# The second expert choice of a routed layer, searched by counting keys on TensorE in 7 rounds

## The chip, the cores and the metric

One core of a Trainium2 chip runs the whole program. The time is the device time of one execution in microseconds (us), as the median of several. The engines are TensorE (PE, with its weight loads shown as PEld), VectorE (DVE), ScalarE (ACT), GpSimd (POOL) and SyncE (SP, which issues most of the transfers). Each engine works through its own instructions strictly in the order in which the program wrote them, and waits on semaphores for the others.

## The reference

Three layers follow each other. Only the second one's choice of tokens matters here.

```python
# attention without softmax, then RMS norm: x of 4608 tokens x 512
logits = x @ w_gate                       # 4608 x 8
order = np.argsort(-logits.flatten())     # all token-expert pairs, best first
for idx in order:
    tok, e = idx // E, idx % E
    if assigned[tok] >= 0 or counts[e] >= cap:   # cap = 4608 / 8 = 576
        continue
    assigned[tok] = e; counts[e] += 1
for e in range(8):
    out[assigned == e] = relu(x[assigned == e] @ w1[e]) @ w2[e]
# third layer, for all tokens: max of three products (each with a relu), then w_out
```

Each expert gets exactly 576 tokens. The kernel never sorts: it settles one expert per "route", eight routes in a row. A route gives every free token its best expert among those still open, finds for each expert how many tokens lie above a threshold, and searches the threshold at which the first expert fills up. That expert takes its tokens and is closed.

## The kernel before

Attention comes first (0 to about 116 us), for all tokens, and leaves the normed tokens in DRAM as `xd` with the logits in SBUF as `L`. Then come eight expert stages. A stage p gathers the 576 tokens of one expert, transposes them, and runs on them w1 (8 tiles of 128 rows, 2 halves of 288 columns), w2 (4 x 2 x 2 halves), the three weights of the third layer (6 x 2 halves x 3) and finally w_out. Every float32 product is made as three matmuls of split operands (function mm3, lines 888 to 890), so a half is 12 matmuls of 288 columns.

Route p+1 runs inside stage p, as a Python generator `phase(p + 1)`. After each half of 12 matmuls the stage calls `tick()`. A tick advances the generator from one `yield` to the next, and so puts a piece of the route's instructions into the queues between two halves. A stage has 68 ticks (the first one 67). `drain()` at its end writes what is left. The order of the instructions on each engine is thus set by where the yields stand. A yield between an instruction on DVE and the one on PE that reads its result gives the DVE a tick's time.

The first stage does one thing more. Its weights of the third layer and w_out arrive as 64-bit words. A second generator, `decoder()`, turns them into float32 pairs, 24 tiles, one piece a tick from the fifth tick on: per tile two ACT casts (lines 367, 368), a shift and a merge on DVE (372, 379), an addition on POOL (380), a cast on ACT (386 or 388) and a subtraction on DVE (394) or POOL (394, 397). The six tiles of w_out are written back to DRAM (`wod`, line 398), and their places then take the last six tiles by a load on SP (line 355). The list `ready` grows to 24 when all is decoded. The buffers `xg` hold both the decoder's values and the gathered tokens, so `tick()` gathers only when `ready` has 24.

The first route (phase 0, before the first stage) searches in `top_search`: DVE compares the keys of all 4608 tokens with 63, 31 or 15 thresholds at once (lines 329, 581, 583), TensorE multiplies the one-hot matrix of experts with these 0/1 columns, 36 pairs of weight load and matmul, and so counts the tokens of each expert above every threshold. A second small matmul spreads the outcome. That takes 7 rounds.

Routes 1 to 6 use `search` (line 504); the last route takes what is left and searches nothing. The keys are first transposed on TensorE (lines 718 to 726) to 96 rows of an expert and a third of the columns. A round has three thresholds. ACT takes two as sums of signs (line 512), DVE the third (514); DVE combines them (518), TensorE sums over rows (523, one small matmul), and DVE compares with the places left and moves the threshold (527 to 534). There are 11 rounds on the upper part of the key, then a change of keys (735 to 743), then 5 rounds on the lower part. A round has two yields, in route 1's first eight rounds three (`slow`).

After the search, `finish` turns the choice into 576 row numbers (IDX; its 36 pairs on TensorE are line 656), `gather` issues five indirect transfers on POOL (line 862), `scale` multiplies the gathered rows with the norm on POOL (868), and `trans` transposes them on TensorE (877). The scaling stands at the stage's end, the transposes among the matmuls of w_out (1044 to 1046), from their second sixth on.

Of the kernel before, what the change touches and what calls it, by code (L numbers as in the profile page):

```python
# [9 lines left out]
F32 = mybir.dt.float32  # L10
F32R = mybir.dt.float32r
BF = mybir.dt.bfloat16
# [11 lines left out]
E = 8  # L24
# [8 lines left out]
J0 = 63  # L33
# [4 lines left out]
def body(ctx: ExitStack, tc: tile.TileContext, qx, kx, vx, g, wg, w1, w2, w123, wo, out):  # L38
# [98 lines left out]
    th0 = ac.tile([128, J0], F32, name="th0")  # L137
    nc.vector.tensor_scalar(th0, d1[:, 1:J0 + 1], 2.0 ** 18, None, op0=OP.mult)
    STEPS = ((2 ** 13, 31), (2 ** 8, 31), (2 ** 4, 15), (1, 15), (16, 15), (1, 15))
    TH = ac.tile([128, 6, 31], F32, name="TH")  # L140
    SV = ac.tile([128, 7], F32, name="SV")
# [361 lines left out]

    def search(KT, i0, i1, REM2, slow):

        T = SC[:, i0]
        for i in range(i0, i1):
# [12 lines left out]
            if slow and i < 8:  # L520
                yield
# [24 lines left out]
    def top_search(g2):  # L546
# [44 lines left out]
        return commit(g2, K, 1.0, OH0)  # L591

# [85 lines left out]

    def phase(p):
# [19 lines left out]
        else:  # L699
# [7 lines left out]
            sf, hi, lo = keys(best, 10)  # L707
            nc.vector.tensor_tensor(sf, sf, hi, op=OP.add)
            nc.vector.tensor_mul(sf, sf, AL)
# [3 lines left out]
            KT = []  # L713
            for i, key in enumerate((sf, best)):
                K = V.rearrange("p e c -> p (e c)").rearrange("p (g e c) -> p g e c", g=3, e=E)
                for g in range(3):
                    gs = slice(12 * g, 12 * g + 12)
                    nc.vector.tensor_mul(K[:, g], oh[:, :, gs], key[:, None, gs].to_broadcast([128, E, 12]))
                yield
                yield  # L720
                pt = rps.tile([128, 512], F32, name="rps")
                for g in range(3):
                    nc.tensor.transpose(pt[0:96, g * 128:g * 128 + 128], K[:, g].rearrange("p e c -> p (e c)"),
                                        ident)
                KT.append(rt.tile([128, 384], F32, name="KT", tag="KT" + str(i))[0:96])
                nc.scalar.copy(KT[i], pt[0:96, 0:384])
                yield
            b1 = None
            for r in search(KT[0], 0, 11, REM2, p == 1):
                if r is None:  # L730
                    yield
                else:
                    b1 = r
            H1 = rt.tile([128, 1], F32, name="H1")
            nc.vector.tensor_scalar(H1, b1, 0.5, None, op0=OP.max)
            nc.vector.scalar_tensor_tensor(KT[1], KT[0], H1[0:96], KT[1], op0=OP.is_equal, op1=OP.mult)
            yield
            nc.vector.tensor_scalar(KT[0], KT[0], H1[0:96], 3000.0, op0=OP.is_gt, op1=OP.mult)
            nc.vector.tensor_add(KT[0], KT[0], KT[1])
            t = rt.tile([128, NT], F32, name="kt")  # L740
            nc.vector.scalar_tensor_tensor(t, sf, H1, best, op0=OP.is_equal, op1=OP.mult)
            nc.vector.tensor_scalar(sf, sf, H1, 3000.0, op0=OP.is_gt, op1=OP.mult)
            nc.vector.tensor_add(sf, sf, t)
            yield
            b2 = None
            for r in search(KT[0], 11, 16, REM2, False):
                if r is None:
                    yield
                else:
                    b2 = r  # L750
            L1 = rt.tile([128, 1], F32, name="L1")
            nc.vector.tensor_scalar(L1, b2, 1.0, None, op0=OP.add)
            flags = commit(g2, sf, L1, oh)
# [158 lines left out]
    beat = 0  # L912

    def tick():
# [183 lines left out]
```

## Time and profile before

| | |
|---|---|
| median of 3 runs | 1275.76 us (1274.73 to 1277.25) |
| profiled execution | 1274.72 us, span 1272.9 us |
| busy PE, DVE, ACT, POOL | 1208.8, 646.0, 482.3, 398.2 us |
| first stage, first matmul of its second half to last of the third layer's | 161.97 to 302.65 us |
| the same stretch, busy PE and DVE | 120.78 and 118.66 us |

Busy time of PE counts matmuls with modelled ends. [...] An idle time in the profile is put down to the instruction that released it. The span lies 1.8 us inside the profiled execution's own time, and that execution is 1.04 us below the median.

### The profile page before, as it was taken

How to read it: one execution, taken by the hardware profiler on the slowest of the kernel's cores; microseconds unless marked ns; L12 is line 12 of the kernel's file. 1: busy time of each engine (PE TensorE's matmuls, PEld its weight loads, DVE VectorE, ACT ScalarE, POOL GpSimd, SP SyncE). 2: the span in 40 equal slices, each digit the busy share in tenths (PEclk: the TensorE clock that was granted, in tenths of full speed). 3: DMA queues.
4: the chain of work that ended last, by engine and by line, in shares of the span. 5: the costliest groups of instructions: out<-in, count | busy, mean ns of one | idle time of the engine just before them, and what ended most of it. 6: DMA issues, size and time to landing. Idle time of an engine off the chain costs nothing.

```text
span 1272.9 us, 23272 instructions
## 1 busy us (share of the span) xinstructions
PE 1208.8 (95%) x8878; PEld 1136.6 (89%) x8880; DVE 646.0 (51%) x2075; ACT 482.3 (38%) x1166; POOL 398.2 (31%) x483
## 2 busy tenths in 40 slices
PE   9996698778999999999999999999999999999996
PEld 7885398777999989998999899999999899989995
DVE  2656688873576346653666167725763421121110
ACT  3547254651453136413542155314631331133110
POOL 0000123544521354135412451245214451253121
PEclk9998798889999999999999999999999999999998
DMA  9999410343330223121311232113312252023101
GB/s 342 396 380 355 150 59 25 118 148 105 109 100 26 80 75 109 34 94 54 102 65 59 64 117 84 59 47 108 100 35 70 76 161 86 1 75 109 59 1 42
DMA packets 52033, 136.15 MB, mean 107 GB/s; under 512 B 5840, under 2 KB 10448, under 8 KB 50384
## 3 DMA queue, kind: packets, MB, share of 16 engines
q1 hardware_dynamic: 44672, 110.25, 25.8%
q0 software_dynamic: 6944, 24.38, 5.7%
q8 instruction: 70, 1.15, 0.4%
q14 instruction: 43, 0.35, 0.1%
q10 hardware_dynamic: 304, 0.02, 0.0%
HBM read 111.43 MB, written 23.20 MB: 106 GB/s over the span
## 4 chain that ended last, share of the span: by engine, by line
PE 77%; DVE 12%; ACT 5%; issue 2%; DMA 2%; POOL 1%; POOLq 0%; SPq 0%; ACTq 0%; DVEq 0%
PE mm L888 19%; PE mm L890 18%; PE mm L889 18%; PE mm L1044 4%; PE mm L1046 4%; PE mm L1045 4%; PE kv L189 4%; ACT W L512 3%; PE o L225 2%; DVE T L534 2%; PE tp L877 1%; DVE w L394 1%; DVE w L379 1%; DVE dv L372 1%; DMA vtb<-vx_dram 1%
## 5 line engine op out<-in xcount | busy, mean ns | idle before, releaser
L888 PE MATMUL mm<-X,w 128*128 128x288 f32 x1152 | 346.9, 301 | 0.0
L890 PE MATMUL mm<-X,w 128*128 128x288 f32 x1152 | 341.3, 296 | 0.0
L889 PE MATMUL mm<-X,w 128*128 128x288 f32 x1152 | 341.2, 296 | 0.0
L888 PEld LDWEIGHTS mm<-X,w 128*128 128x128 f32 x1152 | 218.7, 190 | 0.4
L889 PEld LDWEIGHTS mm<-X,w 128*128 128x128 f32 x1152 | 218.2, 189 | 0.0
L890 PEld LDWEIGHTS mm<-X,w 128*128 128x128 f32 x1152 | 218.0, 189 | 0.0
L838 POOL TENSOR_TENSOR ring<-raw,ring 128x512 fp32r<-128x512 f32 x112 | 144.2, 1289 | 206.8 <-ACT ring L829 195.8
L1021 POOL TENSOR_TENSOR H<-t,H 128x288 fp32r<-128x288 f32 x96 | 77.8, 810 | 417.1 <-ACT H L1020 417.0
L1019 DVE TENSOR_TENSOR t<-mm,t 128x288 f32<-128x288 f32 x192 | 87.1, 454 | 159.5 <-PE mm L890 157.8
L888 PE MATMUL mm<-H,ring 128*128 128x288 f32 x512 | 156.5, 306 | 0.0
L888 PE MATMUL mm<-X,ring 128*128 128x288 f32 (+1 forms) x512 | 153.7, 300 | 1.6 <-ACT X L883 1.6
L889 PE MATMUL mm<-H,ring 128*128 128x288 f32 x512 | 152.3, 297 | 0.0
L890 PE MATMUL mm<-H,ring 128*128 128x288 f32 x512 | 152.1, 297 | 0.0
L890 PE MATMUL mm<-X,ring 128*128 128x288 f32 (+1 forms) x512 | 151.1, 295 | 0.6 <-DVE X L884 0.6
L889 PE MATMUL mm<-X,ring 128*128 128x288 f32 (+1 forms) x512 | 150.7, 294 | 0.0
L512 ACT ACTIVATE W<-KT,T 96x384 bf16<-96x384 f32 x168 | 102.1, 608 | 117.3 <-DVE T L534 117.3
L1020 ACT CAST H<-t 128x288 fp32r<-128x288 f32 x96 | 41.4, 432 | 231.6 <-DVE t L1019 231.6
L888 PEld LDWEIGHTS mm<-X,ring 128*128 128x128 f32 x512 | 96.4, 188 | 2.2 <-ACT X L883 2.1
L888 PEld LDWEIGHTS mm<-H,ring 128*128 128x128 f32 x512 | 98.0, 191 | 0.0
L889 PEld LDWEIGHTS mm<-H,ring 128*128 128x128 f32 x512 | 97.5, 190 | 0.0
L890 PEld LDWEIGHTS mm<-H,ring 128*128 128x128 f32 x512 | 97.2, 190 | 0.0
L890 PEld LDWEIGHTS mm<-X,ring 128*128 128x128 f32 x512 | 96.1, 188 | 1.1 <-DVE X L884 1.1
(257 smaller groups left out, 2037.4 us busy)
## 6 DMA issues: line engine op xcount, KB each, us to landing
raw<-w_dram SPq DMA_DIRECT2D x128, 256.0 KB, 2.7
ring<-wod SPq DMA_DIRECT2D x48, 512.0 KB, 3.5
xd<-y SPq DMA_DIRECT2D x36, 288.0 KB, 9.4
w<-w_dram SPq DMA_DIRECT2D x18, 512.0 KB, 8.2
qta<-qx_dram SPq DMA_DIRECT2D x4, 1280.0 KB, 15.0
qtb<-qx_dram SPq DMA_DIRECT2D x4, 1024.0 KB, 12.4
kta<-kx_dram SPq DMA_DIRECT2D x3, 1280.0 KB, 17.6
vta<-vx_dram SPq DMA_DIRECT2D x3, 1280.0 KB, 16.6
```

Of the source, the lines that this page charges most:

```text
L189: nc.tensor.matmul(KV[b][:, hp, :], KT[bp, o][p0:p1, c - o * CA, h], VT[bp, o][p0:p1, c - o * CA, h], start=(i == 0), stop=(i == len(cs) - 1))
L512: nc.scalar.activation(gs[:, j], KT, AF.Sign, bias=T[0:96, 1 + j:2 + j], scale=-1.0, accum_out=cnt[:, j:j + 1])
L838: (nc.gpsimd if stream[m][0] else nc.vector).tensor_sub(t[:, 1], raw, t[:, 0])
L888: nc.tensor.matmul(ps, wt[:, 0, ws], x[:, 0, xs], start=first, stop=False)
L889: nc.tensor.matmul(ps, wt[:, 1, ws], x[:, 0, xs], start=False, stop=False)
L890: nc.tensor.matmul(ps, wt[:, 0, ws], x[:, 1, xs], start=False, stop=last)
L1019: nc.vector.tensor_tensor(t2, ps[:, :HS], (t1, t1, t2)[j], op=OP.max)
L1020: nc.scalar.copy(m[:, 0, cs], t2)
L1021: nc.gpsimd.tensor_sub(m[:, 1, cs], t2, m[:, 0, cs])
L1044: nc.tensor.matmul(pss[c], l[:, 0, ls], w[:, 0, :], start=(fc == 0), stop=False)
L1045: nc.tensor.matmul(pss[c], l[:, 0, ls], w[:, 1, :], start=False, stop=False)
L1046: nc.tensor.matmul(pss[c], l[:, 1, ls], w[:, 0, :], start=False, stop=(fc == 5))
```

## The change

Route 1 (and it alone) no longer transposes its keys and no longer runs `search`. A new function `count_search` does for it what `top_search` does for the first route: 7 rounds of a compare on DVE, 36 pairs on TensorE, a compare with the places left of each expert (`lim`), a spreading matmul and a reduction. Here a round has two yields between the compare and the count, and two between the count and the spreading matmul. Its first round has 63 thresholds, in two compares with a yield each. The key of route 1 is split 8 bits from the end as in the first route, so `keys` gets 8 in place of 10. The tables of thresholds move to the pool `consts` and become bfloat16. The old code goes as it was into `sign_search`, which routes 2 to 6 still use, without the extra yield.

Besides, `tick()` now gathers in any tick in which no route is left, all is decoded and the last rows are not gathered yet. From the seventh tick after it, it also scales one gathered tile a tick. What is not scaled at the stage's end is scaled there as before.

```diff
+    def count_search(g2, K, L2, oh):
+        ...
+        nc.vector.scalar_tensor_tensor(e8, REM[0:E], 1.0, ident[0:E, 0:E], op0=OP.mult, op1=OP.mult, accum_out=lim)
+        for i in range(7):
+            J = STEPS[i - 1][1] if i else J0
+            ...
+            nt = NT if i else NT // 2
+            for c0 in range(0, NT, nt):
+                ...
+                if ns is None:
+                    nc.vector.tensor_tensor(gs[-1], kc, th, op=OP.is_ge)
+                else:
+                    nc.vector.scalar_tensor_tensor(gs[-1], kc, ns, th, op0=OP.subtract, op1=OP.is_ge)
+                if not i:
+                    yield
+            if ns is not None:
+                nc.vector.tensor_scalar(K, K, ns, None, op0=OP.subtract)
+            yield
+            yield
+            for c in range(NT):
+                nc.tensor.matmul(pc[0:E, 0:J], oh[:, :, c], gs[c // nt][:, c % nt, :], start=(c == 0),
+                                 stop=(c == NT - 1))
+            nc.vector.tensor_scalar(ex[:, 0:J], pc[0:E, 0:J], lim, None, op0=OP.is_gt)
+            yield
+            yield
+            nc.tensor.matmul(pb[:, 0:J], ones8, ex[:, 0:J], start=True, stop=True)
+            nc.vector.scalar_tensor_tensor(sc[:, 0:J], pb[:, 0:J], 0.5, SV[:, i:i + 1].to_broadcast([128, J]),
+                                           op0=OP.is_ge, op1=OP.mult, accum_out=ns)
@@ phase
-            sf, hi, lo = keys(best, 10)
+            sf, hi, lo = keys(best, 8 if p == 1 else 10)
@@ tick
+        for f in fetch:
+            f[1] += 1
+            if f[1] > 6 and f[2]:
+                scale(f[0], f[2].pop(0))
         if route is not None:
             try:
                 next(route)
             except StopIteration:
                 route = None
-                if len(ready) == 24:
-                    gather(len(XG) // 5)
+        if route is None and 0 < len(IDX) < E + 1 and len(XG) < 5 * len(IDX) and len(ready) == 24:
+            fetch[:] = [[len(IDX) - 1, 0, list(range(5))]]
+            gather(len(IDX) - 1)
```

The instructions move as follows. On DVE, at the start of w2 in the first stage, one round stood so before, among the decoder's lines 372, 379 and 394 and the weights' split 838 (X is the half's result, w the decoded tile, T the threshold):

```order
L518 TENSOR_TENSOR ce<-BM,cnt 96x24
L997 TENSOR_TENSOR X<-mm,X 128x288
L394 TENSOR_TENSOR w_4_2352<-dv,w_4_2352 128x512
L372 TENSOR_SCALAR dv<-w_7_961 128x512
L997 TENSOR_TENSOR X<-mm,X 128x288
L838 TENSOR_TENSOR ring<-raw,ring 128x512
L379 SCALAR_TENSOR_TENSOR w_7_961<-w_7_961,dv 128x512
L527 TENSOR_TENSOR ex<-rps,REM_1925 128x24
L529 TENSOR_REDUCE an<-ex 128x3
L531 TENSOR_SCALAR ex,tot<-an 128x3
L534 TENSOR_SCALAR T_2385<-SC,T_2309,tot 128x4
L514 TENSOR_SCALAR W_2388,cnt<-KT,T_2385 96x384
```

and so it stands now, with later line numbers for the same work (903 for 838, 1068 for 997; W is the 0/1 matrix, kf the keys, ns the step that the round found):

```order
L629 TENSOR_SCALAR ex_2398<-rps,lim_2021 8x31
L903 TENSOR_TENSOR ring<-raw,ring 128x512
L379 SCALAR_TENSOR_TENSOR w_6_959<-w_6_959,dv 128x512
L1068 TENSOR_TENSOR X<-mm,X 128x288
L394 TENSOR_TENSOR w_4_2434<-dv,w_4_2434 128x512
L372 TENSOR_SCALAR dv<-w_7_961 128x512
L636 SCALAR_TENSOR_TENSOR scr,ns<-rps,SV 128x31
L617 SCALAR_TENSOR_TENSOR W_2444<-kf,ns,TH 128x540
L621 TENSOR_SCALAR kf<-kf,ns 128x36
L1068 TENSOR_TENSOR X<-mm,X 128x288
L903 TENSOR_TENSOR ring<-raw,ring 128x512
L379 SCALAR_TENSOR_TENSOR w_7_961<-w_7_961,dv 128x512
```

The chain of five dependent instructions from 527 to 514 has gone. In its place stand the reduction 636, one long compare 617 and the subtraction 621, and a tick or two away the short compare 629.

On POOL, at the end of the first stage, the gather (862) and the scaling (868) stood behind the last difference H and the last copy LO of the stage:

```order
L1021 TENSOR_TENSOR H<-t_3388,H 128x288
L1023 CAST LO<-H 128x2x64
L1021 TENSOR_TENSOR H<-t_3467,H 128x288
L1021 TENSOR_TENSOR H<-t_3515,H 128x288
L1023 CAST LO<-H 128x2x64
L862 DMA xg<-xd,idx 128x576 x5
L868 TENSOR_TENSOR xg<-xg 128x4x128 x5
L838 TENSOR_TENSOR ring<-raw,ring 128x512 x4
```

Now the gather stands five differences H before the end and the scaling in two groups among the last ones:

```order
L1092 TENSOR_TENSOR H<-t_3345,H 128x288
L927 DMA xg<-xd,idx 128x576 x5
L1092 TENSOR_TENSOR H<-t_3406,H 128x288
L1094 CAST LO<-H 128x2x64
L1092 TENSOR_TENSOR H<-t_3475,H 128x288
L1092 TENSOR_TENSOR H<-t_3521,H 128x288
L1094 CAST LO<-H 128x2x64
L933 TENSOR_TENSOR xg<-xg 128x4x128 x3
L1092 TENSOR_TENSOR H<-t_3571,H 128x288
L933 TENSOR_TENSOR xg<-xg 128x4x128 x2
L1092 TENSOR_TENSOR H<-t_3620,H 128x288
L1094 CAST LO<-H 128x2x64
```

In the later stages the gather stays where it was, and two of the five scalings move ahead of the last difference H. On TensorE each of the 16 small matmuls of line 523 goes, as do six transposes (723), and seven blocks of 36 pairs (626) with seven small matmuls (633) come, all within the first stage.

## Rows read from the trace of the kernel before

**Rows 1.** Page, part 2: granted clock of TensorE in 40 slices, tenths of full speed
```profile
PEclk9998798889999999999999999999999999999998
```

**Rows 2.** Waits of PE, 140 to 330 us: us in total, times, longest
```profile
PE rps L523 <- DVE ce L518: 18.7, 9, 5.5
```

**Rows 3.** Stretches of first expert: us, busy (x instructions) by engine, PEclk, DMA, GB/s
```profile
161.97:302.65 140.68, 120.78 (x870) 116.91 (x871) 118.66 (x326) 69.30 (x169) 55.45 (x57) 0.93 0.27 92
163.00:284.00 121.00, 101.43 (x698) 98.28 (x699) 104.37 (x274) 65.23 (x160) 51.16 (x50) 0.92 0.27 92
284.00:302.65 18.65, 18.65 (x172) 18.19 (x171) 13.26 (x49) 4.07 (x9) 4.30 (x7) 1.00 0.29 101
```

**Rows 4.** PE's time in order, first expert: start, us, engine, line, op
```profile
185.63 0.29 PE L890 MATMUL mm<-X,ring 128*128 128x288 f32 x1
...
185.76 0.19 PE L523 MATMUL rps<-ce,ones 96*128 96x24 bf16 x1
...
186.02 0.29 PE L889 MATMUL mm<-X,ring 128*128 128x288 f32 x1
```

**Rows 5.** PE's time in order round the 36 pairs of line 656
```profile
297.75 0.29 PE L890 MATMUL mm<-X,w 128*128 128x288 f32 x1
...
297.96 1.07 PE L656 MATMUL rps<-W,W 128*32 128x36 bf16 x36
...
299.21 0.30 PE L889 MATMUL mm<-X,w 128*128 128x288 f32 x1
```

**Rows 6.** Same view as Rows 3, of stretches at the lower clock
```profile
204.00:211.00 7.00, 6.12 (x26) 6.12 (x27) 6.86 (x18) 3.29 (x10) 1.04 (x1) 0.51 0.00 0
234.90:241.70 6.80, 3.65 (x16) 3.65 (x17) 6.38 (x19) 4.06 (x10) 3.02 (x3) 0.50 0.40 135
258.70:262.10 3.40, 3.40 (x17) 3.26 (x16) 2.77 (x7) 1.94 (x6) 3.08 (x4) 0.51 0.54 177
269.00:272.40 3.40, 3.33 (x15) 2.98 (x13) 2.04 (x7) 2.33 (x6) 0.00 (x0) 0.50 1.01 411
```

**Rows 7.** DVE's time in order: one round of the search, and its change of keys
```profile
250.12 0.15 DVE L735 TENSOR_SCALAR H<-T 128x1 f32<-128x1 f32 x1
...
254.78 0.45 DVE L1019 TENSOR_TENSOR t<-mm,t 128x288 f32<-128x288 f32 x1
...
274.72 0.17 DVE L527 TENSOR_TENSOR ex<-rps,REM 128x24 f32<-128x24 f32 x1
...
276.29 0.08 DVE L514 DVE_READ_ACCUMULATOR W<-KT,T 96x1 f32 x1
```

**Rows 8.** DVE by line and form, first expert: xcount | busy us, mean ns
```profile
L518 DVE TENSOR_TENSOR ce<-BM,cnt 96x24 bf16<-96x24 f32 x16 | 4.4, 274 | 2.2 <-ACT W L512 2.2
```

**Rows 9.** Same view, first route, 110 to 157 us
```profile
L583 DVE SCALAR_TENSOR_TENSOR W<-H,ns,TH 128x372 bf16<-128x372 f32 x6 | 3.5, 603 | 0.2
...
L583 DVE SCALAR_TENSOR_TENSOR W<-H,ns,TH 128x180 bf16<-128x180 f32 x6 | 2.3, 404 | 0.5 <-PE rps L585 0.4
...
L329 DVE TENSOR_TENSOR G<-H,th 128x567 bf16<-128x567 f32 x1 | 0.7, 744 | 0.0
```

**Rows 10.** DVE lines 379 and 514, first expert: duration ns min/median/max
```profile
L379 DVE SCALAR_TENSOR_TENSOR w<-w,dv x24: 677/682/1795, 173.0 to 276.7; 128x512 int32<-128x512 int32 x24
...
L514 DVE TENSOR_SCALAR_CACHE_REDUCE W<-KT,T x14: 608/608/610, 189.0 to 275.8; 96x384 bf16<-96x384 f32 x14
```

**Rows 11.** PE's time in order, transposes between first and second expert
```profile
312.37 0.65 PE L877 MATMUL tp<-ident,xg 128*128 128x128 f32 x4 [3.96 <-POOL xg L868]
...
317.20 0.60 PE L877 MATMUL tp<-ident,xg 128*128 128x128 f32 x4
...
320.43 0.60 PE L877 MATMUL tp<-ident,xg 128*128 128x128 f32 x4
```

**Rows 12.** POOL's and ACT's time in order: last store to wod and last reload
```profile
260.80 0.56 POOL L398 DMA_DIRECT2D wod<-w  x1 [0.30 <-POOL w L397]
...
270.07 0.68 ACT L367 ACTIVATE w<-w 128x512 f32<-128x512 f32 x1 [3.19 <-DMA w<-w_dram]
```

More of the change, by code (lines that the diff above doesn't have):

```diff
@@ L136, in body @@
                    allow_small_or_imprecise_dtypes=True)
-    th0 = ac.tile([128, J0], F32, name="th0")
+    th0 = consts.tile([128, J0], BF, name="th0")
     nc.vector.tensor_scalar(th0, d1[:, 1:J0 + 1], 2.0 ** 18, None, op0=OP.mult)
     STEPS = ((2 ** 13, 31), (2 ** 8, 31), (2 ** 4, 15), (1, 15), (16, 15), (1, 15))
-    TH = ac.tile([128, 6, 31], F32, name="TH")
-    SV = ac.tile([128, 7], F32, name="SV")
+    TH = consts.tile([128, 6, 31], BF, name="TH")
+    SV = consts.tile([128, 7], F32, name="SV")
     for i, (stp, J) in enumerate(STEPS):
@@ L502, in bc, with search @@
         return ap[:, :, None].to_broadcast([128, E, NT])
-    def search(KT, i0, i1, REM2, slow):
+    def search(KT, i0, i1, REM2):
         T = SC[:, i0]
@@ L706, in phase @@
                 yield
[L707 removed]
+            sf, hi, lo = keys(best, 8 if p == 1 else 10)
             nc.vector.tensor_tensor(sf, sf, hi, op=OP.add)
[L709 removed]
+            if p == 1:
+                nc.vector.scalar_tensor_tensor(sf, sf, 1.0, AL, op0=OP.add, op1=OP.mult)
+                nc.vector.tensor_scalar(sf, sf, -1.0, None, op0=OP.add)
+            else:
+                nc.vector.tensor_mul(sf, sf, AL)
             nc.vector.tensor_scalar(best, lo, 1.0, None, op0=OP.add)
@@ L712, in phase @@
             yield
[L713 to L750, printed above, removed]
@@ L751, in phase @@
-            L1 = rt.tile([128, 1], F32, name="L1")
-            nc.vector.tensor_scalar(L1, b2, 1.0, None, op0=OP.add)
-            flags = commit(g2, sf, L1, oh)
+            flags = None
+            if p == 1:
+                for r in count_search(g2, sf, best, oh):
+                    if r is None:
+                        yield
+                    else:
+                        flags = r
+            else:
+                flags = yield from sign_search(g2, V, sf, best, oh, REM2)
         yield
@@ L912, in body @@
     beat = 0
+    fetch = []
     def tick():
@@ L1024, in body @@
         drain()
-        if (p + 1, 0) not in XG and p + 1 < E:
-            gather(p + 1)
         if p + 1 < E:
-            for c in range(5):
-                scale(p + 1, c)
+            if (p + 1, 0) not in XG:
+                gather(p + 1)
+                fetch[:] = [[p + 1, 0, list(range(5))]]
+            while fetch[0][2]:
+                scale(p + 1, fetch[0][2].pop(0))
         odd = p % 2
```

68 lines of the change are left out of this document (66 added, 2 removed).

## The prediction

> **What bounds the kernel now.** I read the page first. TensorE is busy for 95% of the span, and its granted clock falls below nine tenths only in the fourth, fifth and seventh to ninth of 40 slices, the first route and the first expert stage [rows 1]. So I looked at the list of waits there. TensorE waits 18.7 us, in nine waits of up to 5.5 us, for the product ce (line 518), the last step on VectorE before each small matmul of the search [rows 2]. A last wait of 3.96 us stands at the first transpose for the second expert, released by the scaling on POOL [rows 11]. The table by stretches sizes the first stage: from 161.97 to 302.65 us TensorE is busy 120.78 of 140.68 us and idle 19.9; VectorE is busy 104.37 of the 121 us from 163 to 284, while the decoder runs, and 13.26 of 18.65 after it [rows 3]. In the decoder's part VectorE has far more work than the rest of the kernel gives it, and the route's steps queue behind the decoder's. So I take the stage as bound by VectorE's queue there, and by TensorE after it.
>
> The clock adds to the idle time. [...] At the full level they follow each other by 0.13 us (185.63 to 185.76) [rows 4]; I use 0.133, as 12 of them take 1.6 us. 74 of them would take 9.84 us in place of 16.50, so the clock costs 6.65 us, a third of what the idle time costs.
>
> **TensorE's part of the sum.** Without idle time and low clock the stretch would have taken 120.78 - 6.65 = 114.1 us. The change removes 16 small matmuls. From 185.63 to 186.02 us two matmuls and a small one take 0.39 us, so a small one costs 0.39 - 2 x 0.133 = 0.12 us, and 16 cost 2.0 [rows 4]. Six transposes go too; I leave their gain, under 1 us, uncounted. What comes is 7 x 36 pairs. Line 656 has such a block of 36 columns in the same stage: from 297.75 to 299.21 us it stands with two matmuls, so it costs 1.46 - 0.27 = 1.19 us [rows 5]. Rounds of 15 and 31 columns should cost no more, and that of 63 not much more: its upper bound is 36 whole matmuls of 288 columns, 4.8 us, and I take 1.19. Seven blocks are 8.3 us, seven spreading matmuls at 0.12 are 0.85. TensorE gains 7.2 us of work, and its floor for the stretch is 121.3 us: at most 140.7 - 121.3 = 19.4 us to win.
>
> [...]
>
> **VectorE's part.** A round of the search occupies it from 274.72 to 276.29 us, 1.57 us; 16 rounds are 25.1. The change of keys occupies 250.12 to 254.78, less 0.6 for a decoder step within it: 4.1. The products ce are 4.4 [rows 7, 8]. The six products before the transposes go too (uncounted). So 33.6 us go. The compares come. In the first route 372 elements took 603 ns and 180 took 404, that is 1.036 ns an element [rows 9]. The compare without a step took 744 ns for 567. By this: 1134 elements 1.33 us, twice; 1116 with a step 1.37, twice; 540 with a step 0.78, three times; 540 without 0.72. Together 8.5 us. Some 21 short steps (compares with the limit, reductions, subtractions) at about 0.2 us, as the short steps of a round now, are 4.2. Net, VectorE loses 20.9 us of work. ACT loses its 32 sums of signs and the waits of its queue for the thresholds, and gains nothing.
>
> The shorter route also moves: 50 yields in place of 67 bring the choice's end (finish) from behind the decoder into its part. That adds to the decoder's part on VectorE the 13.26 us of the tail without its eight own maxima of 0.45: 9.7 us [rows 3, 7]. So VectorE has 104.4 - 20.9 + 9.7 = 93.2 us there. TensorE's floor for that part is 101.43 - 6.65 + 7.2 + 1.7 (line 656 and its followers move in) = 103.7 us [rows 3, 5]. Before, VectorE was busy 104.4 of 121 us, 86%, while TensorE waited for it. Some of its own gaps went to ACT's casts, which stood behind the sums of signs, and those go; so I take that it can be filled to 88%. There is a second cost. The decoder's merge takes 677 ns at best, 1795 at worst, and the third threshold of the old search never more than 610 [rows 10]. The merge reads two tensors as the new compares do, so the compares will be held up like it; at its mean excess of 0.16 us eight compares cost 1.3 us. With 94.5 us at 88% the part takes 107.4 us, 3.7 over TensorE's floor. With a third more for the clock that is 4.9 us left of the waits. If VectorE could be filled wholly it is 0; at 80% with all compares held by a full 1.1 us it is 102.2 / 0.8 = 127.8, 24 us over and 32 with the clock; that is the other bound, by which the stage would lose 13.
>
> [...]
>
> **The stage's end.** The gather waited for the route's last tick, and the scaling for the gather. With 17 yields less the decoder, not the route, decides: its 51 pieces begin at the fifth tick, so it ends at about the 55th of 67. The gather then has 12 ticks of 1.6 us, the scaling starts seven ticks later, and both are done when the transposes begin. That removes 3.96 us of wait. The first two transposes stand 4.83 us apart, the next two 3.23, and the low clock behind the wait is what differs: 1.6 us more [rows 11]. Cover for it is POOL's spare time: after the decoder it is busy 4.30 of 18.65 us [rows 3], and 10 us of gather and scaling fit. Without the cover the 5.6 us come back.
>
> Edits at nothing: thresholds in bfloat16 leave the keys in float32, so I take the first route's compares as unchanged; they are 3.5 + 2.3 us there, and half or twice of that, 2.9 us less or 5.8 more, are the bounds [rows 9]. In later stages two scalings of 1 us move ahead of the last difference H on POOL, which TensorE needs only in the last sixth of w_out, over 10 us later. SP's loads for the second expert wait for the route's choice, which now comes earlier; they are hidden now and stay so.
>
> **The sum.** 19.4 - 4.9 + 5.6 = 20.1 us. The profiled execution took 1274.72 us, so 1254.6. It lies 1.04 us below the median of the runs, so I predict 1255.7 us for the median.
>
> **The rivals.**
> 1. No waits are left: TensorE's floor holds, and the 4.9 us and up to 1 for the transposes are won as well: 1250. For it: by the sum VectorE has 9 us of slack in the decoder's part. Against: order within a queue never fills it wholly.
> 2. The reloads take over. The last store to `wod` is issued at 260.80 us and ACT starts on the reloaded tile at 270.07, 9.3 us later, after a wait of 3.19 [rows 12]. The program leaves four ticks between. They now last 6.4 us and no longer 9, so ACT waits 2.9 us for each of the last three such tiles, 2.9 to 8.7 in all, and VectorE's maxima wait behind ACT's copies. At the middle 5.8 us come back: 1261.5. Against: TensorE runs ahead on six result buffers.
> 3. The early gather doesn't hide, for its buffers are the decoder's: 5.6 us come back, 1261.
> 4. VectorE stays the bound, its compares held up as the merge is at worst: half of the far bound, 12 us over in place of 3.7, with a third for the clock 16: 1267.
> 5. Slower. Each of the seven rounds has two places where TensorE can wait (before the count and before the spreading), two ticks behind the VectorE step that feeds it. If VectorE lags by more than these 3.2 us, all 14 wait. At the old mean of 18.7 / 9 = 2.1 us and a third for the clock that is 39 us [rows 2]: 1250 + 39 = 1289. It decides against the change from 1.3 us a wait on. Against: the sum leaves VectorE slack.
> 6. The waits go to another reader in the same queue, and nothing is gained: 1275.
>
> **How the numbers follow.** Forecast 0.58, rivals 0.12, 0.12, 0.05, 0.07, 0.04 and 0.02. The forecast's own range is 1251 to 1260 (VectorE filled to between 92 and 86%: 0 to 6.2 us over the floor, 0 to 8.2 with the clock). With rivals 1 to 3 in full and half of 4 the range is 1247 to 1267. A measurement of this kernel tells about 0.2%, 2.6 us. Faster by more: 0.94; the same: 0.02; slower: 0.04.
>
> **What would show it.** The list of waits should have no wait for ce in the first stage, and in its place a few us, each below 2, at the count (line 626) or the spreading (633). The table by stretches should show the granted clock near 1 there, VectorE near 88% while the decoder runs, and the seven blocks of pairs at 1.2 us each. The wait for the scaling (line 933) should be gone. Wrong would be: a block above 2 us, nine or more waits over 2 us at the new matmuls, ACT's wait for the reloads of 6 us or more with TensorE waiting behind it, or a change in the later stages.

## The result, and the profile after

| | before | after |
|---|---|---|
| median of 3 runs | 1275.76 us | 1263.27 us (1261.94 to 1265.01) |
| ratio | | 0.9902 (0.9877 to 0.9927) |
| profiled execution, span | 1274.72, 1272.9 us | 1265.01, 1263.2 us |
| first stage, first matmul of 320 columns to last of the third layer | 140.68 us | 133.26 us |
| from there to the fifth group of transposes | 24.35 us | 18.66 us |
| first matmul of 320 columns begins at | 161.97 us | 164.98 us |

The kernel is 12.5 us faster; the forecast was 20.1, and the 1255.7 us predicted lie 7.6 below the time. The two profiles differ by 9.7 us of span: 7.4 won in the stage, 5.7 at its end, 3.0 lost ahead of it, and 0.4 lost in the rest. The execution that was profiled after is the slowest of its three.

The table by stretches shows the stage of the changed kernel, to be read against the first line of [rows 3] (stretch; its length; busy time with the count of PE, PEld, DVE, ACT and POOL; granted clock; DMA share; GB/s):

```profile
164.98:298.24 133.26, 124.45 (x1107) 120.48 (x1108) 105.64 (x225) 49.13 (x103) 69.44 (x67) 0.96 0.32 109
164.98:236.00 71.02, 69.72 (x698) 66.81 (x699) 63.30 (x131) 27.34 (x59) 29.60 (x24) 1.00 0.19 60
236.00:282.00 46.00, 38.50 (x290) 37.42 (x289) 39.02 (x88) 18.56 (x38) 27.53 (x29) 0.89 0.53 190
...
236.00:270.00 34.00, 26.50 (x201) 25.42 (x200) 31.37 (x68) 13.91 (x28) 21.09 (x22) 0.86 0.37 126
249.97:253.38 3.41, 3.41 (x16) 3.41 (x15) 3.31 (x8) 3.41 (x8) 2.60 (x3) 0.50 0.00 0
263.62:270.45 6.83, 5.82 (x47) 5.37 (x44) 5.45 (x14) 2.91 (x6) 3.31 (x3) 0.50 0.43 139
```

Three things stand in it. TensorE is busy 124.45 of 133.26 us, so it is idle 8.81, where it was idle 19.9. The search, which now ends at about 236 us, costs it almost nothing: idle 1.30 of 71.02 us. And the part after it has become the bad one: from 236 to 270 us TensorE is busy 26.50 of 34.00 while VectorE is busy 31.37, 92%. The last two lines are the stretches at the lower level (granted clock 0.50) that follow there. 9.23 us of matmuls at half clock cost 4.6 us.

The list of waits names what TensorE waited for (140 to 330 us; in total, times, longest). It stands against [rows 2]:

```profile
PE rps L705 <- DVE W L699: 3.2, 2, 2.2
PE rps L664 <- DVE tots L656: 3.1, 2, 2.7
...
PE rps L827 <- DVE c L821: 1.6, 1, 1.6
...
PE rps L626 <- DVE W L615: 0.7, 1, 0.7
PE rps L626 <- DVE W L617: 0.6, 2, 0.3
```

No wait for ce is left, and the counts of line 626 wait 1.3 us in all. The others are the route's tail: the count of ties (827), the totals (664) and the one-hot blocks (705) (the short one of the two waits at 664 is the first route's). In order of time, TensorE's rows with the idle time before each:

```profile
241.73 0.17 PE L827 MATMUL rps<-c,ones 128*128 128x16 bf16 x1 [1.62 <-DVE c L821]
...
249.50 0.18 PE L664 MATMUL rps<-tots,tri 128*128 128x1 bf16 x1 [2.71 <-DVE tots L656]
...
263.15 0.63 PE L705 MATMUL rps<-W,W 128*32 128x36 bf16 x18 [2.17 <-DVE W L699]
264.79 0.72 PE L705 MATMUL rps<-W,W 128*32 128x36 bf16 x18 [1.01 <-DVE W L699]
```

These four are 7.5 of the 8.81 us. The transposes after the stage, against [rows 11], stand 3.23 us apart from the first on, and none waits for the scaling:

```profile
303.88 0.60 PE L942 MATMUL tp<-ident,xg 128*128 128x128 f32 x4
...
307.11 0.60 PE L942 MATMUL tp<-ident,xg 128*128 128x128 f32 x4
```

The blocks of 36 pairs, which [rows 5] priced, took 1.05 to 1.30 us, and the longest is the one of 63 columns:

```profile
179.91 1.30 PE L626 MATMUL rps<-W,oh 128*8 128x63 bf16 x36
...
188.02 1.07 PE L626 MATMUL rps<-W,oh 128*8 128x31 bf16 x36
```

### The profile page after: what moved, and what is told of

It is laid out like the page before. It is cut to its first block, busy times and chain, and to the rows that moved or that the text cites. A ratio compares the mean times of both kernels' runs of the same rounds, so it can differ in the third digit from the quotient of the medians.

```text
span 1263.2 us, 23578 instructions
## 1 busy us (share of the span) xinstructions
PE 1213.0 (96%) x9117; PEld 1141.6 (90%) x9117; DVE 633.2 (50%) x1974; ACT 462.2 (37%) x1100; POOL 402.3 (32%) x483
## 4 chain that ended last, share of the span: by engine, by line
PE 80%; DVE 12%; ACT 3%; issue 2%; DMA 2%; POOL 0%; SPq 0%; POOLq 0%; DVEq 0%; ACTq 0%
PE mm L953 20%; PE mm L955 19%; PE mm L954 19%; PE mm L1116 4%; PE mm L1118 4%; PE mm L1117 4%; PE kv L189 3%; PE o L225 2%; ACT W L512 2%; DVE T L532 1%; PE tp L942 1%; DMA vta<-vx_dram 1%; DVE dv L372 1%; DMA vtb<-vx_dram 1%; PE rps L705 1%
## 5 line engine op out<-in xcount | busy, mean ns | idle before, releaser
L512 ACT ACTIVATE W<-KT,T 96x384 bf16<-96x384 f32 x140 | 85.1, 608 | 87.4 <-DVE T L532 87.4
L953 PEld LDWEIGHTS mm<-X,ring 128*128 128x128 f32 x512 | 96.9, 189 | 2.2 <-ACT X L948 2.0
L955 PEld LDWEIGHTS mm<-X,ring 128*128 128x128 f32 x512 | 96.6, 189 | 0.5 <-DVE X L949 0.5
L953 PEld LDWEIGHTS mm<-H,ring 128*128 128x128 f32 x512 | 96.7, 189 | 0.2
L954 PEld LDWEIGHTS mm<-X,ring 128*128 128x128 f32 x512 | 96.8, 189 | 0.0
L954 PEld LDWEIGHTS mm<-H,ring 128*128 128x128 f32 x512 | 96.4, 188 | 0.0
```

The costliest lines, as they stand in the source:

```text
L512: nc.scalar.activation(gs[:, j], KT, AF.Sign, bias=T[0:96, 1 + j:2 + j], scale=-1.0, accum_out=cnt[:, j:j + 1])
L953: nc.tensor.matmul(ps, wt[:, 0, ws], x[:, 0, xs], start=first, stop=False)
L954: nc.tensor.matmul(ps, wt[:, 1, ws], x[:, 0, xs], start=False, stop=False)
L955: nc.tensor.matmul(ps, wt[:, 0, ws], x[:, 1, xs], start=False, stop=last)
```

## The experiments

Each of the fourteen rows has a profile of its own; "stage" and "end" are the two stretches of the table above. Idle is TensorE's in the stage, clock its mean granted clock there, as a share of full speed. Medians are of 3 to 12 runs, the ratio is to runs of the kernel before on the same chip.

| kernel | median us | ratio (95%) | start | stage | idle | clock | end |
|---|---|---|---|---|---|---|---|
| before | 1275.76 | | 161.97 | 140.68 | 19.9 | 0.93 | 24.35 |
| before again | 1277.79 | 0.9996 (0.9987 to 1.0005) | 164.90 | 140.64 | 22.8 | 0.95 | 24.39 |
| after | 1263.27 | 0.9902 (0.9877 to 0.9927) | 164.98 | 133.26 | 8.8 | 0.96 | 18.66 |
| after again | 1263.27 | 0.9883 (0.9866 to 0.9899) | 164.88 | 133.42 | 8.9 | 0.96 | 18.65 |
| search only | 1270.30 | 0.9940 (0.9926 to 0.9954) | 164.24 | 132.96 | 8.2 | 0.96 | 24.11 |
| schedule only | 1277.28 | 1.0001 (0.9991 to 1.0011) | 164.73 | 143.77 | 22.5 | 0.94 | 18.63 |
| tail spread | 1261.09 | 0.9872 (0.9856 to 0.9887) | 163.23 | 130.12 | 7.7 | 0.99 | 18.65 |
| counts doubled | 1268.07 | 0.9926 (0.9913 to 0.9939) | 163.36 | 138.14 | 7.0 | 0.96 | 18.65 |
| GpSimd cut | 1253.01 | 0.9800 (0.9782 to 0.9818) | 164.30 | 121.89 | 1.8 | 1.00 | 18.64 |
| low parts on ScalarE | 1263.74 | 0.9889 (0.9871 to 0.9906) | 164.54 | 132.31 | 8.0 | 0.96 | 18.64 |
| subtractions on VectorE | 1261.59 | 0.9874 (0.9856 to 0.9891) | 163.12 | 130.26 | 8.1 | 0.99 | 18.65 |
| output weights early | 1264.97 | 0.9896 (0.9881 to 0.9911) | 164.78 | 134.30 | 9.4 | 0.96 | 18.65 |
| early and spread | 1263.56 | 0.9888 (0.9874 to 0.9903) | 164.19 | 131.86 | 8.2 | 0.97 | 18.66 |
| early, spread, VectorE | 1260.21 | 0.9864 (0.9849 to 0.9879) | 163.43 | 129.83 | 6.5 | 0.97 | 18.65 |

The theory after the first profile was that the missing part of the gain went into TensorE's waits for the route's tail. Its rival was that VectorE's whole load bounds the stage, wherever the tail stands. A side question was the start, 3.0 us later than before.

**After again.** No edit.

> The changed kernel once more, for its time beside the runs of this call and for a second profile. Time: 1262 to 1265 us. The open point is the stage's start, which in the first profile came 3.0 us later than before (first matmul of 320 columns at 164.98 us, 161.97 before). If that is chance of the clock (a stretch at half clock at 157.6 to 164.4 fell on the first projections), this profile or those of the other kernels, which run the same instructions up to there, show it at 162 to 163 in some; if the change makes it, it stands at 164.5 to 165.5 in every one of them.

It measured 1263.27 us, and its profile repeats the first to 0.2 us. Its four executions fell in two groups, 1261.9 and 1262.2 us at a mean clock of 0.983, 1264.4 and 1265.1 at 0.979, and both profiles are of the second sort. So executions differ by some 2.6 us, the shorter ones at the higher mean clock; where in the execution that lies isn't shown, as neither profile is of the first sort. The start was at 163.1 to 163.4 us in four of the later profiles and at 164.2 to 165.0 in the rest: later than 161.97 in all of them, but not always by 3 us. That left both readings open.

**Before again**, for the start. No edit.

> The kernel before once more, for a second profile of its start. In its first profile the first matmul of 320 columns began at 161.97 us; in all nine profiles of kernels with the change or a part of it, the second route's search left as it was among them, it began at 163.1 to 165.0, and in each of these a stretch at half clock of 3.4 or 6.8 us lay on the first projections. If the later start is the change's, this profile shows 161.5 to 162.5 and no half clock after 156 us; if it is chance in the gather's landing and the clock, it shows 163 to 165 here too. Time: the same as before, ratio within 0.2% of 1.

The kernel before started at 164.90 us this time. TensorE's rows show why (start; duration; idle time before it):

```profile
156.39 2.13 PE L877 MATMUL mm<-ident,xg 128*128 128x128 f32 x8 [4.37 <-issue]
159.30 0.58 PE L888 MATMUL mm<-X,ring 128*128 128x256 f32 x1 [0.78 <-ACT X L883]
...
164.90 0.41 PE L888 MATMUL mm<-X,ring 128*128 128x320 f32 x1 [0.85 <-ACT X L883]
```

TensorE stood idle 4.37 us before the transposes of the first gathered rows, where the first profile shows 0.86 us, and the first 256-column matmuls then took 0.41 us for the most part, against 0.28. In after's profile, too, they took 0.41 us, at a granted clock of 0.50 (158.57 to 161.66 us). So the late start comes without the change too. How often before starts late isn't shown: one of its two profiles does, and so do all twelve of the changed kernel and its variants. Against this profile, which starts like after's, the span is 13.1 us shorter: 7.4 in the stage and 5.7 at its end. The medians give much the same: the eleven runs of before beside "after again" have 1277.41 us, 14.1 more than it.

**Search only**, the counts on TensorE with gather and scaling where they were:

```diff
-        for f in fetch:
-            ...
             except StopIteration:
                 route = None
-        if route is None and 0 < len(IDX) < E + 1 and len(XG) < 5 * len(IDX) and len(ready) == 24:
-            ...
-            gather(len(IDX) - 1)
+                if len(ready) == 24:
+                    gather(len(XG) // 5)
```

(and at the stage's end the gather, if it is still due, and all five scalings, as before)

> The search is counted on TensorE, but gather and scaling go back to where they were: the gather only where the route ends with the decoder done, else at the stage's end. The decoder ends after the route (tick 57 against 50), so the gather comes at the end. First theory (the end's 5.6 us are owed to the gather within the ticks): 1269 us, the transposes 4 to 5 us apart again and one wait of about 4 us for the scaling on GpSimd. Rival (gather and scaling within the ticks take as much from the decoder and VectorE as they give at the end): 1263 us, as the changed kernel.

Its median is 7.0 us over after's, and its profiled span 4.8. The end alone is 5.45 us longer, and its transposes look as before; the stage began 0.7 us earlier and took 0.3 less:

```profile
306.97 1.11 PE L942 MATMUL tp<-ident,xg 128*128 128x128 f32 x4 [3.96 <-POOL xg L933]
...
311.53 0.60 PE L942 MATMUL tp<-ident,xg 128*128 128x128 f32 x4
```

The stage is as long as in after (132.96 us), so gather and scaling within the ticks take nothing from the decoder. The first theory held.

**Schedule only**, the old search without its extra ticks, gather and scaling within the ticks:

```diff
-            if p == 1:
+            if p == E:
                 for r in count_search(g2, sf, best, oh):
```

(and `keys(best, 10)` again, with the old product by AL)

> The other part alone: the second route searches in 16 rounds of sign sums again, without the eight extra ticks of before, and the gather and scaling come within the ticks as in the changed kernel. The route ends at tick 59 of 67, the scalings then fall due at ticks 66 to 70, so most of them at the stage's end. First theory (the counts carry the 7.4 us of the stage, the early gather the 5.5 us at its end): 2 to 4 us of the end are won and none of the stage, 0.997 to 0.999 of before, with waits on L523 of 17 us or more. Rival (the shorter schedule is what gains): 0.992 or less of before. Second rival (the eight ticks spaced the rounds, without them they wait more): slower than before, 1.001 or more, with waits on L523 over 22 us.

The time did not move (1.0001 of before), so none of the three expectations held. The end is won in full, 5.7 us, more than I had given it, but the stage is 3.1 us longer than before. The list of waits shows that the old search still waits 16.6 us, and that the totals of the tail now wait too, which stand beside the decoder's end here:

```profile
PE rps L521 <- DVE ce L518: 16.6, 11, 4.5
PE rps L664 <- DVE tots L656: 3.3, 2, 3.1
```

So the schedule alone gains nothing, and the counts carry the gain of the stage. Some 1.7 us came later in this kernel's profile, behind the second expert's first transposes; I did not follow them.

**Counts doubled.** Each block of pairs is issued twice. The second pass begins with `start` at its first pair, as the first does, and the run gives each expert the same tokens. So its sums are made anew and the counts stay as they were, though the expectation takes them to come out double:

```diff
-            for c in range(NT):
+            for _ in range(2):
+                for c in range(NT):
```

> Each block of 36 small count matmuls in the second route is issued twice into the same sums (so the counts come out double and the tokens chosen are others). That adds 7 x 36 matmuls, 1.05 to 1.30 us a block, 7.7 us on TensorE, none on VectorE. First theory (TensorE sets the time where the counts are, VectorE the tail): the counts' ticks grow by all of it, 1270 to 1272 us. Rival (VectorE sets the time through the whole stage): TensorE's added work fits into its waits, 1263 to 1266 us.

It cost 4.8 us by the medians and 4.9 by the stage, between the two expectations. A doubled block of 63 columns took 2.43 us, one of 31 columns 1.99:

```profile
178.64 2.43 PE L627 MATMUL rps<-W,oh 128*8 128x63 bf16 x72
...
187.87 1.99 PE L627 MATMUL rps<-W,oh 128*8 128x31 bf16 x72
```

Seven of them add 1.13 + 6 x 0.92 = 6.7 us, 1 less than I had taken, and TensorE's busy time in the stage rose by just that (131.17 against 124.45 us). Its idle time fell by 1.8 us; the other 4.9 lay on the path. So TensorE sets the time in the search for most of what was added, as the forecast had it, and not the tail alone.

**Tail spread**, seven more ticks ahead of the tail's matmuls:

```diff
+        for _ in range(2 if p == 1 else 0):
+            yield
         pc = rps.tile([128, 512], F32, name="rps")
```

(the same ahead of po and pi, one tick ahead of pk)

> Seven more ticks within the second route's tail: two ahead of the matmul on c2, two ahead of the one on tots, two ahead of the 36 one-hot matmuls, one ahead of the last four. First theory (the part of the gain that is missing went into TensorE's waits for the tail, 7.5 us at 241 to 265, and into the stretches at half clock that follow them, 3.41 and 6.83 us long, worth some 5): waits on L705, L664 and L827 in the second route fall to under 2 us together, the half clock goes with them, 1253 to 1257 us; the gather comes 0 to 3 ticks later and one or two scalings move to the stage's end at 1 us each. Rival (VectorE's load in the decoder's part sets the time, and a wait taken away here returns elsewhere): 1262 to 1265 us, with waits of 6 us or more at other lines.

2.2 us were won, not 6 to 10; 1261.09 lies between the two expectations. The waits on 827 and most of 705 went, but 2.2 us stayed at the totals and 2.4 came at the last step:

```profile
PE rps L725 <- DVE R L715: 2.4, 1, 2.4
PE rps L666 <- DVE tots L656: 2.2, 1, 2.2
```

Idle time fell by 1.1 us only; what the stage won beyond that is clock (0.99 against 0.96, and after's profile is of one of its longer executions). Part of the waits came back elsewhere, as the rival said, though not the 6 us that it named. With more ticks TensorE had something to do, and VectorE was late again at a later step.

**Low parts on ScalarE**, to take load off VectorE ahead of the tail. ScalarE copies the piece where VectorE subtracted, so the low parts are not made:

```diff
-            (nc.gpsimd if stream[m][0] else nc.vector).tensor_sub(t[:, 1], raw, t[:, 0])
+            if stream[m][0] or m < 3:
+                (nc.gpsimd if stream[m][0] else nc.vector).tensor_sub(t[:, 1], raw, t[:, 0])
+            else:
+                nc.scalar.copy(t[:, 1], raw)
```

> For 13 pieces of the first expert's weights ScalarE copies the raw piece where VectorE subtracted (the low parts are wrong then): 13 x 0.75 = 9.7 us less on VectorE, 13 x 0.62 = 8 us more on ScalarE, all in the first two thirds of the stage, before the route's tail. First theory (TensorE's waits are made in the tail, by what stands in VectorE's queue there): the search part was at 97% to 99% of TensorE already, so 0 to 1.5 us are won, 1261.5 to 1263.5 us, and the waits of the tail stay at 7 to 8 us. Rival (VectorE's sum over the whole stage is the bound): the waits fall by most of 9.7 us, 1254 to 1257 us.

VectorE's busy time in the stage fell from 105.64 to 94.45 us, and the time did not move (1263.74). The tail's waits are the same to 0.1 us (that at 664 is 2.7 us here too):

```profile
PE rps L705 <- DVE W L699: 3.2, 2, 2.2
...
PE rps L827 <- DVE c L821: 1.6, 1, 1.6
```

That fells the rival in its plain form. VectorE's load over the stage is not what counts; what counts is what stands in its queue in the 34 us of the tail.

**GpSimd cut**, its two operations of the decoder on 32 of 512 columns. It leaves the rest of the decoded weights unmade, so it is a measurement and not a version to use:

```diff
-        nc.gpsimd.tensor_tensor(XV[i], up, r, op=OP.add)
+        nc.gpsimd.tensor_tensor(XV[i][:, 0:32], up[:, 0:32], r[:, 0:32], op=OP.add)
-            nc.gpsimd.tensor_sub(w[:, 512:1024].bitcast(F32R), v, w[:, 0:512].bitcast(F32))
+            nc.gpsimd.tensor_sub(w[:, 512:544].bitcast(F32R), v[:, 0:32], w[:, 0:32].bitcast(F32))
```

> GpSimd's two operations in the decoder (24 integer additions of 1.18 us and 6 subtractions of 1.46 us in the stage) work on 32 of 512 columns, so the decoded weights are wrong in the rest; nothing else changes. First theory (in the route's tail VectorE is held up by GpSimd: L372, L675, L646, L839 and others took 9.4 us more there than their usual times, and VectorE waited 10.4 us in the stage for decoder copies that stand behind GpSimd's additions): the waits on L827, L664 and L705 fall by half or more and their half-clock stretches with them, 1254 to 1258 us, and L372 stays under 0.5 us each time. Rival (it is VectorE's own load and the order of its queue): L372 is quick, but the waits stay within 2 us of 7.5, 1261 to 1264 us.

1253.01 us, 10.3 under after. The tail's waits at 827, 664 and 705 were gone; one of 1.1 us came at its last step (719), where after has none:

```profile
PE rps L719 <- DVE R L711: 1.1, 1, 1.1
```

The stage took about what TensorE needs for it:

```profile
164.30:286.19 121.89, 120.11 (x1107) 116.40 (x1107) 88.01 (x225) 48.90 (x103) 44.92 (x67) 1.00 0.35 119
236.00:270.00 34.00, 32.72 (x277) 31.97 (x276) 25.42 (x75) 17.29 (x35) 14.77 (x26) 1.00 0.60 222
```

VectorE did the same 225 instructions in 88.01 us in place of 105.64. Only GpSimd's two operations differ, so the other 17.6 us of its busy time in after are hold-ups, as I call the time by which an instruction lasts longer beside GpSimd's work; the profile counts it as busy. In after's tail they read so, first on VectorE (start; duration; operation):

```profile
247.21 0.25 DVE L838 SCALAR_TENSOR_TENSOR TIE<-M,dx,gt 128x36 f32<-128x36 f32 x1
247.38 1.09 DVE L839 SCALAR_TENSOR_TENSOR A<-M,dx,gt 128x36 f32<-128x36 f32 x1
...
249.29 0.15 DVE L656 TENSOR_SCALAR tots<-sA 128x1 bf16<-128x1 f32 x1
...
251.63 1.32 DVE L675 SCALAR_TENSOR_TENSOR kp<-sT,of,TIE 128x36 f32<-128x36 f32 x1
...
253.16 0.45 DVE L1090 TENSOR_TENSOR t<-mm,t 128x288 f32<-128x288 f32 x1
253.53 2.83 DVE L372 TENSOR_SCALAR dv<-w 128x512 int32<-128x512 int32 x1
```

and at the same times on GpSimd:

```profile
247.37 1.04 POOL L380 TENSOR_TENSOR dv<-w 128x512 int32<-128x512 int32 x1 [2.00 <-DVE w L379]
...
251.62 1.28 POOL L397 TENSOR_TENSOR w<-dv,w 128x512 fp32r<-128x512 f32 x1
253.20 0.56 POOL L398 DMA_DIRECT2D wod<-w  x1 [0.30 <-POOL w L397]
253.78 1.05 POOL L380 TENSOR_TENSOR dv<-w 128x512 int32<-128x512 int32 x1
254.78 1.29 POOL L397 TENSOR_TENSOR w<-dv,w 128x512 fp32r<-128x512 f32 x1
```

Line 839, a product of 36 columns, begins with GpSimd's addition (380) and ends with it; its neighbour 838 of the same size took 0.25 us. Line 675 begins and ends with GpSimd's subtraction (397). Line 372, usually 0.42 us, stands for 2.83 us, through the issue of a store, an addition and a subtraction in a row. With GpSimd cut the same steps took:

```profile
242.21 0.28 DVE L839 SCALAR_TENSOR_TENSOR A<-M,dx,gt 128x36 f32<-128x36 f32 x1
...
245.67 0.29 DVE L675 SCALAR_TENSOR_TENSOR kp<-sT,of,TIE 128x36 f32<-128x36 f32 x1
...
246.53 0.46 DVE L372 TENSOR_SCALAR dv<-w 128x512 int32<-128x512 int32 x1
```

```profile
246.20 0.56 POOL L398 DMA_DIRECT2D wod<-w  x1 [0.30 <-POOL w L397]
```

The issue of a store stands beside line 372 here too, and it took 0.46 us. So it is the addition and the subtraction that held it in after, and not the store.

Over the tail, seven such steps of the route (lines 646, 647, 832, 839, 675, 692, 699) are 6.0 us longer in after than here, and two of line 372 are 3.2 us longer. One step went the other way: line 693 took 0.82 us in after and 1.42 here. VectorE's waits for the decoder's copies are no part of it: they rose from 10.4 to 16.1 us in this kernel, and TensorE did not notice.

Not every step is held. Durations in after's stage, lowest, median and highest in ns:

```profile
L372 DVE TENSOR_SCALAR dv<-w x19: 411/420/2829, 192.8 to 275.8; 128x512 int32<-128x512 int32 x19
```

```profile
L1090 DVE TENSOR_TENSOR t<-mm,t x20: 435/449/458, 230.4 to 288.9; 128x288 f32<-128x288 f32 x20
```

The maximum of line 1090 was never held, though it ran beside the same GpSimd work (at 264.66 us, for one, in 0.44 us, beside an addition from 264.15 us on). What sets it apart from line 372, no run shows.

**Subtractions on VectorE**, the six of line 397:

```diff
-            nc.gpsimd.tensor_sub(w[:, 512:1024].bitcast(F32R), v, w[:, 0:512].bitcast(F32))
+            nc.vector.tensor_sub(w[:, 512:1024].bitcast(F32R), v, w[:, 0:512].bitcast(F32))
```

> The six subtractions of the output weights' decoding (L397) move from GpSimd, where each took 1.46 us, to VectorE, where the same shape takes 0.7 (L394's usual time). First theory (GpSimd's operations hold VectorE up, by about 1 us each in the tail): 6 x 0.7 = 4.2 us added, 5 to 7 us of longer durations gone, and the additions behind them on GpSimd come earlier, so that VectorE's waits for decoder copies shrink: 1259 to 1262 us. Rival (VectorE's own load counts): 4 us more on a VectorE that is 92% busy there, 1265 to 1268 us.

1261.59 us, as the first theory had it. With six instructions more VectorE is busy 103.00 us in the stage, 2.6 less than in after. They add 6 x 0.7 = 4.2 us, so 6.8 us of hold-ups went, 1.1 for each: here a subtraction on GpSimd cost VectorE more than doing it itself. TensorE's idle time fell by 0.7 us only (1.3 us of it now stand at 719), and the clock was better, 0.99 against 0.96.

**Output weights early**, the same work at another place:

```diff
-    ORDER = [0, 1, 2, 3, 4, 5, 6, 7, 8, 18, 9, 19, 10, 20, 11, 21, 22, 23] + list(range(12, 18))
+    ORDER = [0, 1, 2, 3] + list(range(18, 24)) + list(range(4, 18))
```

(and the loads of the words follow this order)

> The changed kernel with another order of the decoder: the six output-weight pieces, whose low parts GpSimd subtracts (1.46 us each) and stores, are decoded as 5th to 10th piece in place of 10th to 18th, so that these subtractions run at about ticks 18 to 28, beside the search, and not in the route's tail; the others follow in order. Leaving GpSimd's operations out nearly altogether won 10 us. First theory (what costs is that GpSimd's subtraction and addition stand back to back where TensorE waits for a short chain of the tail): the waits on L827, L664 and L705 of the second route fall from 7.5 to 3 to 4 us, few come at L626, 1257 to 1261 us. Rival (they cost the same wherever they run): waits of 3 us or more at L626 and L633, 1262 to 1265 us. Second rival (weights of the third layer come too late): TensorE waits at the third layer's matmuls, 1266 us or more.

1264.97 us: nothing won. The waits moved to the counts, which wait 3.9 us in place of 1.3, and the totals still wait. The likely reason, not tested by itself, is that the additions stay in the tail:

```profile
PE rps L664 <- DVE tots L656: 3.2, 2, 2.7
...
PE rps L626 <- DVE W L617: 2.0, 3, 1.2
...
PE rps L626 <- DVE W L615: 1.9, 1, 1.9
```

The rival held: GpSimd's operations cost about the same here, in the search or in the tail, wherever a chain of the route ran beside them (1264.97 us against after's 1263.27).

**Early and spread**, both edits together:

> That order of the decoder and the seven more ticks in the tail together. First theory (both act on the same waits, from two sides): 1255 to 1259 us, with under 3 us of waits in the tail. Rival (the seven ticks won 2.2 us and the order the rest, and nothing adds up, since VectorE has no room there): no better than the better of the two alone, 1259 to 1262 us.

1263.56 us: no better than "tail spread" alone (1261.09), and above the rival's 1259 to 1262 too. That nothing adds up, as the rival said, held.

**Early, spread, VectorE**, with the subtractions on VectorE too:

> The same, and the six subtractions on VectorE as well (0.7 us each there). First theory (GpSimd's operations beside VectorE are what costs, and six of 30 are gone): 1254 to 1258 us, 1 to 2 us under the version without. Rival (VectorE has 97% to 99% of TensorE beside it in the search and no room for 4 us more): 1258 to 1262 us, with waits at L626.

1260.21 us (1259.43 to 1261.88), the lowest median of the kernels that compute everything, within the rival's 1258 to 1262 and not the 1254 to 1258 of the first theory; the waits at 626 are 1.3 us, as in after. Its interval (0.9849 to 0.9879) overlaps that of "after again" (0.9866 to 0.9899); "tail spread" took 1260.08 to 1261.98 us against its 1261.9 to 1265.08. "Tail spread" and "subtractions on VectorE" came within 1.4 us of it with one edit each. That these versions beat the kernel before by 16 to 18 us is clear of the spread; that they beat after, by 2 to 3 us, is likely and no more.

## Why the prediction was nearly right

The direction held, and the time was 7.6 us off. 1263.27 lies in the stated range of 1247 to 1267, but above the forecast's own 1251 to 1260. It lies nearest to rivals 2 and 3 (1261.5 and 1261), which did not come, so that the wide range held is in part luck. By the steps:

- **What bounds the stage.** Right: VectorE's queue, and TensorE beneath it. With GpSimd's operations cut beside VectorE the stage came down to within 1.8 us of TensorE's floor; load taken off VectorE ahead of the tail did not count.
- **TensorE's floor, 121.3 us.** Right to 1.2 us. In "GpSimd cut" the stage took 121.89 with 1.8 idle, at full clock, so the floor is 120.1. The 6.65 us that the prediction takes off for the clock are those of [rows 6] and [rows 4]: 74 matmuls busy for 16.50 us at a granted clock of 0.50 to 0.51, less 74 x 0.133 us. Blocks at 1.19 us were 1.05 to 1.30; 36 pairs of 31 columns took 1.07 us, and 36 more of them 0.92 us, 26 ns each.
- **VectorE's compares.** Nearly right: 1134 elements took 1.32 us (1.33 predicted), 540 took 0.78 and 0.72 (0.78 and 0.72), 1116 took 1.38 and, held, 2.19 (1.37).
- **The residual waits, 4.9 us. This step failed.** "With 94.5 us at 88% the part takes 107.4 us, 3.7 over TensorE's floor. With a third more for the clock that is 4.9 us left of the waits." Measured: 8.8 us idle and 4.3 to 4.6 for the clock (the busy time over "GpSimd cut" and half of the 9.23 us at half clock), 13.3 in all. The mean of 88% was right; from 164.98 to 282 us VectorE was busy 102.3 of 117.0, 87%. But a mean hides the place. In the search VectorE was at 89% and TensorE lost 1.3 us in 71. In the tail VectorE was at 92% and TensorE lost 7.5 us in 34. Each count has two ticks behind its compare, and the tail's steps form one chain, but that this cover makes the difference isn't shown: more ticks in the tail won 2.2 us, and with GpSimd's subtractions beside them the counts waited 3.9 us for all their cover. I had priced the tail's 9.7 us from where it stood before, behind the decoder, with GpSimd at 4.30 of 18.65 us. Where it moved to, GpSimd was busy 21.09 of 34 and made seven of its steps 6.0 us longer. By the sum VectorE would have been busy 118.66 - 20.9 + 1.3 = 99.1 us in the stage; it was 105.64. I had seen the hold-up in [rows 10] and charged it to the compares alone. The trace of before shows it on other lines too, line 394 with up to 2.73 us for one step; in "GpSimd cut" no step of this line was held (durations of before, then of "GpSimd cut"; lowest, median and highest in ns):

```profile
L394 DVE TENSOR_TENSOR w<-dv,w x14: 673/694/2727, 197.7 to 283.5; 128x512 fp32r<-128x512 f32 x14
```

```profile
L394 DVE TENSOR_TENSOR w<-dv,w x14: 680/692/694, 201.0 to 270.6; 128x512 fp32r<-128x512 f32 x14
```

- **The clock.** A third of the idle time was too little: 4.3 to 4.6 on 8.8 is half. The mean clock also differs between executions of the changed kernel, 0.979 to 0.983.
- **The stage's end, 5.6 us.** Right: 5.7 by the profiles, 5.45 by "search only".
- **The rivals.** Number 4 (the compares held up as the merge is at worst) saw hold-ups and put them at the wrong steps, and so at 1267 with 0.07; that GpSimd makes them, "GpSimd cut" showed, with 17.6 us less busy time on VectorE. Number 2 is seen on ScalarE alone: it waited 4.7 us for one reloaded tile, and no matmul waited behind it. Number 6 came in part: 7.5 us of waits stand at other readers of VectorE's queue. Numbers 1, 3 and 5 did not come. Number 1's 1250 is what "GpSimd cut" came within 3 us of. The signs that the prediction names look at the new matmuls (626, 633) and not at the tail's (827, 664, 705), where the waits came.
- **The base.** The sum was made against one execution of before. Its second profile started 2.9 us later, and its later runs have medians of 1277.4 to 1278.1. Beside "after again" the gain is 14.1 us, 6.0 short of the forecast.

What stays open: how the 10 us that "GpSimd cut" won divide between the 24 additions and the six subtractions. Moving the subtractions won 1.7, and no run left out the additions alone.

## What to carry to other kernels

When a change moves a chain of short steps, price it by what runs on the other engines at its new place, not by its durations at the old one; here seven steps took 6.0 us longer there beside GpSimd. A mean busy share hides the place: near 90% VectorE cost TensorE 1.3 us in 71 in one part of this stage and 7.5 in 34 in the next. Before you rearrange ticks, look for short instructions whose duration equals that of a GpSimd instruction beside them, as 1.09 us (line 839) beside 1.04 and 1.32 us (line 675) beside 1.28: those may be hold-ups, though the profile counts them as work. Here cutting GpSimd's instructions showed that they were, for the two then took 0.28 and 0.29 us.

## What the runs showed of the hardware

A single VectorE instruction was held through several GpSimd instructions in a row: line 372 took 2.83 us in place of 0.42 while an addition and a subtraction ran (253.78 to 256.07 us). And the price of a further pair of weight load and small matmul reads best from two lengths of a block: 36 pairs of 31 columns took 1.07 us and 72 took 1.99, so 36 more cost 0.92 us, 26 ns each. At 63 columns they took 1.30 and 2.43, so 31 ns each. A single block divided by its pairs (30 and 36 ns) comes out higher. A matmul of the blocks lasts 0.17 to 0.20 us (line 626), and 35 times 26 ns with one matmul of 0.18 us make up the 1.07 us.
